# Gated linear recurrence and an ELU layer on one core: running products of decays with one score product per chunk, in place of a tree over queries and keys

## The chip, the cores and the metric

The kernel runs on one core of a Trainium2 chip. The metric is the device time in microseconds (us), as a median of runs; lower is better. Engines: PE is TensorE's matmul, PEld its weight load, DVE is VectorE, ACT is ScalarE, POOL is GpSimd, SP is SyncE, which issues the transfers.

## The reference

Four batches, eight heads, 768 tokens, a head of 48. A complex state per head decays by a complex factor at each token and takes up an outer product; the query reads its real part. The 3072 results of 384 then pass through a layer with an ELU and 2048 hidden columns. Inputs are float32, but the two weights come as float64, which the kernel turns into float32 itself.

```python
mag = np.sqrt(a_re * a_re + a_im * a_im)
scale = np.minimum(mag, 0.999) / (mag + 1e-06)
a_re_n, a_im_n = (a_re * scale, a_im * scale)
# ... cut: states start at zero
for t in range(S):
    ar, ai = (a_re_n[:, :, t, :, None], a_im_n[:, :, t, :, None])
    new_re = ar * S_re - ai * S_im
    new_im = ar * S_im + ai * S_re
    kv = np.einsum('bhd,bhe->bhde', k[:, :, t], v[:, :, t])
    S_re, S_im = (new_re + kv, new_im)
    y[:, :, t] = np.einsum('bhd,bhde->bhe', q[:, :, t], S_re)
# ... cut: x is y with heads side by side
h = x @ w_in
g = np.where(h > 0.0, h, alpha * (np.exp(np.minimum(h, 0.0)) - 1.0))
return (g @ w_out).astype(np.float32)
```

## The kernel before

Twelve groups of 256 tokens, two chunks of 128 each. Inside a chunk, a query at t and a key at s meet in exactly one block of 2, 4, .. 128 tokens that has s in its left half and t in its right half. At each of seven levels the kernel makes scores for those pairs, then widens queries (on DVE) and keys (on POOL) by the decays of the neighbouring block. Nothing is divided, so any decay is right.

```python
def product(eng, x, y_re, y_im, to_re, to_im, sign, shape, tag, seen=lambda t: t):
    # ... cut: buffers t1 and t2, signs
    eng.tensor_tensor(out=t1, in0=x, in1=y_re, op=ALU.mult)
    eng.tensor_tensor(out=t2, in0=x, in1=y_im, op=ALU.mult)
    eng.tensor_tensor(out=to_re, in0=seen(t1[:, 0]), in1=seen(t2[:, 1]), op=minus)
    eng.tensor_tensor(out=to_im, in0=seen(t1[:, 1]), in1=seen(t2[:, 0]), op=plus)

def widen(x, h):
    # ... cut: views of the chunk by blocks of h tokens
    product(nc.vector, qv, tot(0, 0), tot(1, 0), qv[:, 0], qv[:, 1], 1, shape, "pq")
    # ... cut: a new buffer for keys
    product(
        nc.gpsimd, old[:, :, 0], tot(0, 1), tot(1, 1), to[:, 0, 0], to[:, 1, 0], -1,
        shape, "pk", seen,
    )
    for i in range(2):
        nc.scalar.copy(out=to[:, i, 1], in_=seen(old[:, i, 1]))
    x["K"] = new

# ... cut: the order of a group; `behind` holds the ELU layer of the group before it
        for l, h in enumerate(LEVELS):
            for x in xs:
                scores(x, h)
                widen(x, h)
                if l % 2 or h == LEVELS[-1]:
                    values(x, l // 2)
            for w in weights[:4]:
                load_weights(*w)
            # ... cut
            if behind:
                behind.pop(0)()
```

## Time and profile before

| | before |
|---|---|
| time, median of the first 3 runs | 1701.91 us (1699.12 to 1703.77) |
| granted PE clock of the profiled run, mean | 0.819 |
| time per group of 256 tokens | 132 us, or 0.515 us a token |
| matmul records on PE | 10464 |
| table loads on ACT | 21 |

The page cuts the span into 40 equal slices, each digit being tenths of a slice in which the engine was busy. These are three engines' lines of the page of the kernel before:

```profile
PE   3522368948848847866876874894893893894989
...
DVE  7897888788788777867868868858858858858831
...
POOL 6574464665465464544654654645545645635610
```

A PE that alternates between 9 and 3 or 4 is one that stops once in every group. DVE is mostly at 7 or 8 and POOL at 4 to 6.

### The profile page before, as it was taken

To read this page: it belongs to the slowest core of one execution; us is meant where nothing else is said; L and a number is where in the kernel's file an instruction comes from. 1 tells how busy PE (TensorE), PEld (TensorE's weight loads), DVE (VectorE), ACT (ScalarE), POOL (GpSimd) and SP (SyncE) were. 2 spreads that over 40 slices of the span, in tenths; PEclk is the share of its full clock that TensorE was granted. 3 is DMA by queue.
4 is the path that set the end of the run, shared out by engine and by line. 5 is a ranking of instruction groups with operands and counts; after the bars stand their busy time and mean duration, and the time that the engine had idled before them with its cause. 6 is when DMAs were issued, how large, how long until landed. Compare 5 with 4: busy or idle time off the path is not lost.

```text
span 1704.6 us, 26958 instructions
## 1 busy us (share of the span) xinstructions
PE 1193.1 (70%) x10464; PEld 922.5 (54%) x10464; DVE 1289.6 (76%) x1860; ACT 439.2 (26%) x865; POOL 893.2 (52%) x835
## 2 busy tenths in 40 slices
PE   3522368948848847866876874894893893894989
PEld 2521355637637636655654653663662763773766
DVE  7897888788788777867868868858858858858831
ACT  2010043124124123122322331331421521311313
POOL 6574464665465464544654654645545645635610
PEclk8555679778978978987996996996895996996999
DMA  5413330030031040022022013013012012010000
GB/s 108 107 54 108 116 60 11 18 72 17 18 67 26 18 76 16 15 59 37 12 51 49 12 47 51 8 38 65 8 38 54 20 34 45 13 33 23 2 19 10
DMA packets 156895, 69.67 MB, mean 41 GB/s; under 512 B 134496, under 2 KB 142432, under 8 KB 156768
## 3 DMA queue, kind: packets, MB, share of 16 engines
q1 hardware_dynamic: 156768, 67.94, 17.8%
q8 instruction: 84, 1.38, 0.4%
q14 instruction: 43, 0.35, 0.1%
HBM read 36.44 MB, written 4.72 MB: 24 GB/s over the span
## 4 chain that ended last, share of the span: by engine, by line
PE 45%; DVE 44%; issue 4%; POOL 3%; ACT 2%; DMA 1%; SPq 1%; POOLq 0%; DVEq 0%
PE bank L414 15%; PE a L277 11%; DVE pq L248 8%; DVE pq L247 8%; PE bank L397 8%; PE y L304 6%; DVE T L250 4%; DVE T L251 4%; DVE Q L251 3%; DVE Q L250 3%; DVE r L192 3%; DVE a_sb L288 2%; DVE g L406 2%; POOL wp L172 2%; DVE Q L224 2%
## 5 line engine op out<-in xcount | busy, mean ns | idle before, releaser
L277 PE MATMUL a<-Q,K 48*64 48x128 f32 (+1 forms) x4992 | 350.6, 291 | 334.7 <-DVE Q L250 291.3
L277 PEld LDWEIGHTS a<-Q,K 48*64 48x64 f32 x4992 | 307.1, 149 | 387.5 <-issue 275.9
L250 POOL TENSOR_TENSOR K<-pk,pk 128x256 f32<-128x256 f32 x168 | 145.0, 863 | 408.0 <-PE a L277 400.4
L397 PE MATMUL bank<-x,w_in 128*128 128x256 f32 x1152 | 305.3, 421 | 13.2 <-ACT er L404 8.9
L332 ACT COPY K<-K 128x256 f32<-128x256 f32 x336 | 137.5, 445 | 566.6 <-PE a L277 492.1
L397 PEld LDWEIGHTS bank<-x,w_in 128*128 128x128 f32 x1152 | 232.9, 209 | 66.1 <-issue 22.8
L414 PE MATMUL bank<-w_out,g 128*128 128x384 f32 x768 | 267.0, 501 | 0.1
L247 POOL TENSOR_TENSOR pk<-K,T 128x512 f32<-128x512 f32 x168 | 208.6, 1242 | 67.8 <-DVE T L250 50.4
L248 POOL TENSOR_TENSOR pk<-K,T 128x512 f32<-128x512 f32 x168 | 231.0, 1375 | 0.0
L250 DVE TENSOR_TENSOR Q<-pq,pq 128x256 f32<-128x256 f32 x168 | 109.5, 652 | 131.7 <-PE a L277 126.0
L414 PEld LDWEIGHTS bank<-w_out,g 128*128 128x128 f32 x768 | 143.7, 193 | 98.9 <-issue 11.2
L304 PE MATMUL y<-a_sb,vl 128*64 128x128 f32 (+1 forms) x1344 | 119.5, 316 | 98.3 <-DVE a_sb L288 98.3
L248 DVE TENSOR_TENSOR pq<-Q,T 128x512 f32<-128x512 f32 x168 | 174.7, 1040 | 0.0
L247 DVE TENSOR_TENSOR pq<-Q,T 128x512 f32<-128x512 f32 x168 | 166.6, 992 | 3.9
L304 PEld LDWEIGHTS y<-a_sb,vl 128*64 128x64 f32 (+1 forms) x1344 | 94.3, 163 | 134.3 <-DVE a_sb L288 115.5
L406 DVE SCALAR_TENSOR_TENSOR g<-ee,er 128x512 f32<-128x512 f32 x96 | 85.5, 893 | 89.8 <-ACT ee L405 89.8
L251 POOL TENSOR_TENSOR K<-pk,pk 128x256 f32<-128x256 f32 x168 | 149.0, 887 | 0.0
L251 DVE TENSOR_TENSOR Q<-pq,pq 128x256 f32<-128x256 f32 x168 | 131.8, 785 | 0.0
L288 DVE TENSOR_TENSOR a_sb<-a,masks 128x1024 f32<-128x1024 f32 x72 | 87.4, 1214 | 55.7 <-PE a L277 55.7
L403 ACT ACTIVATE ee<-bank 128x512 f32<-128x512 f32 x96 | 57.1, 595 | 234.0 <-PE bank L397 179.6
L247 DVE TENSOR_TENSOR pq<-T 128x512 f32<-128x512 f32 (+6 forms) x168 | 100.5, 598 | 17.5 <-ACT T L219 12.4
L248 DVE TENSOR_TENSOR pq<-T 128x512 f32<-128x512 f32 (+6 forms) x168 | 97.3, 579 | 0.0
(68 smaller groups left out, 1261.2 us busy)
## 6 DMA issues: line engine op xcount, KB each, us to landing
w<-in_moe_w_in_dram SPq DMA_DIRECT2D x12, 512.0 KB
vl<-vn SPq DMA_DIRECT2D x48, 128.0 KB
vl<-vn SPq DMA_DIRECT2D x96, 64.0 KB
vl<-vn SPq DMA_DIRECT2D x192, 32.0 KB
w<-in_moe_w_out_dram SPq DMA_DIRECT2D x16, 384.0 KB
ar<-in_a_re_dram SPq DMA_DIRECT2D x24, 192.0 KB
ai<-in_a_im_dram SPq DMA_DIRECT2D x24, 192.0 KB
kn<-in_k_dram SPq DMA_DIRECT2D x24, 192.0 KB
```

The source lines that it names most:

```text
L247: eng.tensor_tensor(out=t1, in0=x, in1=y_re, op=ALU.mult)
L248: eng.tensor_tensor(out=t2, in0=x, in1=y_im, op=ALU.mult)
L250: eng.tensor_tensor(out=to_re, in0=seen(t1[:, 0]), in1=seen(t2[:, 1]), op=minus)
L251: eng.tensor_tensor(out=to_im, in0=seen(t1[:, 1]), in1=seen(t2[:, 0]), op=plus)
L277: nc.tensor.matmul(x["a"][ts(row, HP), z, ts(p, n)], lhsT=x["K"][rows, i, ts(p, C // 2)], rhs=x["Q"][rows, i, ds((p + 1) * C - n, n)], sta ...
L288: nc.vector.tensor_tensor(out=a, in0=x["a"].rearrange("p j (x t) -> p j x t", t=C), in1=masks[:, n].unsqueeze(1).unsqueeze(1).to_broadcast ...
L304: nc.tensor.matmul(to, **got, start=False, stop=False, skip_group_check=True)
L332: nc.scalar.copy(out=to[:, i, 1], in_=seen(old[:, i, 1]))
L397: nc.tensor.matmul(t[:, e], lhsT=w_in[:, i, ts(f0 + f + e, C)], rhs=x[:, i], start=(i == 0), stop=(i == NI - 1),)
L403: nc.scalar.activation(out=e, in_=t, func=AF.Relu, scale=-1.0)
L406: nc.vector.scalar_tensor_tensor(out=g[:, f : f + 2], in0=e, scalar=-1.0, in1=r, op0=ALU.add, op1=ALU.add)
L414: nc.tensor.matmul(t, lhsT=gs[f // FB][:, f % FB, ts(c, C)], rhs=w_out[:, f], start=(f == 0), stop=(f == NF - 1),)
```

## The change

The intent is to replace the tree by running products. Within a group of now 384 tokens the kernel computes P, the product of all decays up to each token (divided by powers of 0.905, the middle of the expected range, so that it stays near 1). The decay between s and t is P at t over P at s. Queries are multiplied by P, keys divided by it, and one ordinary 96 by 96 score product per head and chunk replaces seven levels. Three neighbouring tokens lie on one partition: P is first multiplied within the triples, then over 128 triples by a doubling scheme in transposed form (`across`), then turned back (`back`).

Division is only safe while P stays in range. The kernel therefore looks at the squared size of P at every eighth triple, keeps the smallest and the largest, and after the loop a branch runs a plain token-by-token version if either left its bounds. Other parts of the change: all products move to DVE, POOL keeps one addition per weight tile and some small fills, and 1/|a| is made by Ln and Exp instead of Sqrt and a reciprocal.

```diff
-C = 128  # tokens of a chunk, the length over which decays are multiplied out
-LEVELS = [1, 2, 4, 8, 16, 32, 64]
+J = 3
+NB = 128
+GT = J * NB
+CB = 32
+C = J * CB
+BASE = 0.905
 # ... cut: normalising, of a third of a group (j)
-        nc.scalar.activation(out=m, in_=m, func=AF.Sqrt)
-        nc.vector.reciprocal(out=r, in_=r)
+                nc.scalar.activation(out=y, in_=s, func=AF.Ln)
+                nc.scalar.activation(out=y, in_=y, func=AF.Exp, scale=-0.5)
+                nc.scalar.activation(out=t, in_=y, func=AF.Square)
+                nc.scalar.activation(out=s, in_=y, func=AF.Ln, scale=2.0 / CAP * EPS, bias=1.0)
+                nc.scalar.activation(out=s, in_=s, func=AF.Exp, scale=-1.0)
 # ... cut: running products over 128 triples, four DVE instructions per level and block
-    def widen(x, h):
+            def across(levels):
+                Z = x["Z"]
+                for h in levels:
+                    o = Z[:, :, :, 1:].rearrange("p i m (n s b) -> p i m n s b", s=2, b=h)
+                    for m in range(NI):
+                        product(r, tot, r, shape, "u")
+            def back():
+                nc.vector.tensor_tensor(out=low, in0=low, in1=s[:, 0], op=ALU.min)
+                nc.vector.tensor_tensor(out=high, in0=high, in1=s[:, 0], op=ALU.max)
+                X = nat["X"] = sb.tile(flat, FP32, tag="X", name="X")
+                for i in range(2):
+                    t = bank([NB, HD])
+                    for m in range(NI):
+                        nc.tensor.transpose(t[:, ts(m, 128)], Z[:, i, m, 0:NB], ident)
+                    nc.scalar.mul(out=X[:, i], in_=t, mul=place)
 # ... cut: queries_keys(j): queries times P, keys times conj(P) / |P|^2, both transposed
-    def scores(x, h):
+        def attend(x, c, state, y_sb, last):
+                    nc.tensor.matmul(
+                        sc[:, e], lhsT=K[:, h + e, ts(c, C)], rhs=Q[:, h + e, ts(c, C)],
+                        start=True, stop=True,
+                    )
 # ... cut: the order of a group; `behind` is the ELU layer of the group before,
 # `ahead` the preparation of the next one, in four chunks of which the last is `late`
+                late = c == NC - 1
+                for s in behind if late else behind[:5]:
+                    s()
+                behind = behind[5:]
+                for s in ahead if late else ahead[:3]:
+                    s()
+                ahead = ahead[3:]
 # ... cut: at the end
+    general(tc, cst, ident, w_in, w_out, low, high, q, k, v, a_re, a_im, out)
```

## The prediction

> **What bounds the kernel now.** I read the page's head first, for the load of each engine, then its chain, then groups kept apart by shape, and last stretches of the timeline.
>
> ```profile
> PE 1193.1 (70%) x10464; PEld 922.5 (54%) x10464; DVE 1289.6 (76%) x1860; ACT 439.2 (26%) x865; POOL 893.2 (52%) x835
> ...
> PEclk8555679778978978987996996996895996996999
> ...
> PE 45%; DVE 44%; issue 4%; POOL 3%; ACT 2%; DMA 1%; SPq 1%; POOLq 0%; DVEq 0%
> ```
>
> No engine is full. The chain that ends last is half TensorE (PE) and half VectorE (DVE): they hand work to each other level by level, and PE's granted clock drops while it waits. The groups by shape:
>
> ```profile
> L277 PE MATMUL a<-Q,K 48*64 48x128 f32 x4224 | 319.6, 302 | 334.7 <-DVE Q L250 291.3 <-DVE Q L224 28.0 <-DVE Q L251 14.8
> L248 DVE TENSOR_TENSOR pq<-Q,T 128x512 f32<-128x512 f32 x168 | 174.7, 1040 | 0.0
> L248 POOL TENSOR_TENSOR pk<-K,T 128x512 f32<-128x512 f32 x168 | 231.0, 1375 | 0.0
> ```
>
> The third number after the bar is idle time ahead of the group and who ended it: PE idles 335 us ahead of the tree's scores, 291 of it for DVE's query products. Why those are slow shows in three timeline rows of DVE:
>
> ```profile
> 43.65 0.69 DVE L247 TENSOR_TENSOR pq<-T 128x512 f32<-128x512 f32 x1
> 384.00 0.15 DVE L251 TENSOR_TENSOR T<-pq,pq 128x4 f32<-128x4 f32 x1
> 399.25 1.75 DVE L248 TENSOR_TENSOR pq<-Q,T 128x512 f32<-128x512 f32 x1
> ```
>
> The same 512 elements take 0.69 us while GpSimd (POOL) is idle and 1.75 us while it works on keys. The two clean rows give a law: 0.15 us + 1.04 ns per element (384: 0.55 us, as the state row of the last group has). The period of the loop is in the chain in order of time; the rows are three groups of 256 tokens apart:
>
> ```profile
> 479.06 1.93 PE y L343 x32
> ...
> 874.82 1.93 PE y L343 x32
> ...
> 1270.84 1.93 PE y L343 x32
> ```
>
> That is 396 us for three, 132 us a group, 0.515 us a token.
>
> **What the Trainium skill says.** (1) "SBUF — State Buffer": the port pair that DVE and GpSimd share is an exclusive lock, and a DVE instruction with two SBUF inputs contends with a GpSimd one that reads SBUF. The trace agrees (0.69 against 1.75 us). (2) "ScalarE: Activation LUTs", What ACT_TABLE_LOAD costs: about 1283 ns, plus a drain of 1380 ns. The trace has 21 loads of 1283 ns, but the next activation starts at once, so I count 1.28 us. (3) The same page, Table sets: one set holds Exp and Ln. The changed build's instruction listing nevertheless has a load between almost every Ln and Exp. (4) "TensorE: Matmul & The Clock Gate", Part 1: idling halves the PE clock. The trace agrees: 16 value matmuls take 1.09 us warm and 1.95 us after an idle time of 4.7 us.
>
> **The change, part by part.** Counts are from the listing of the two builds' instructions. A float32 matmul appears in the trace as two records.
>
> *Removed.* All 24 trees: 4992 score records (64 take 3.69 us warm, so 288 us of PE), 1536 value records, DVE's query products and POOL's key products (168 x 4 each), 336 key copies on ACT, 12 reciprocals of 4.94 us, and 528 small transfers that sort values. POOL keeps only 34 additions in the weight conversion, about 45 us instead of 893. So from the first group on, DVE has the lock to itself.
>
> *PE after.* The two MLP products stream the same columns: 768 + 768 records of 384 columns, 32 of them in 10.52 us, so 0.329 us each, 253 + 253 us. Attention: 512 score records of 96x96, 448 state updates, 512 values, 448 state reads. From the warm paces of similar shapes (0.036 to 0.064 us where halves of the array alternate; I take 0.1 us where the whole array is used) this is 51 + 40 + 26 + 22 us. 480 transposes at 0.136 us (8 in 1.09) are 65 us. Sum 710 us warm, 89 us in each of eight groups of 384 tokens.
>
> *DVE after,* by the law: 40 complex products of 768 (3.0 us each) 120; 168 products of 128 along the chunk totals (1.0 us) 168; normalising 24 x 3.15 = 76; the rest of queries and keys 24 x 4.1 = 98; masks, states and elu, 220 of 384 elements, 121; weights 34 conversions 88; rest 8. Sum 679 us instead of 1290: 74 us a group, and the weights once.
>
> *ACT after.* Activations by the rows of before (768: 0.84, 512: 0.585, 384: 0.48 us) 349 us; table loads: 137 outside the token-by-token path, x 1.28 = 176 us. Sum 525, 66 us a group; up from 439.
>
> *Stages.* The listing fixes each engine's order, so I walk it.
> - Prologue, nothing beside it: loads 5; normalising, bound by ACT with its loads, 25; products within triples 6; transposes 2; 21 chained products 20; back 2; queries and keys 26. About 86 us.
> - First group: DVE carries its 63 us and some 25 weight conversions of 2.7 us: 130 us.
> - A middle group has three phases. Attention with normalising: ACT has some 37 us (nine to ten loads, 12 of the MLP's tiles), 38 with handoffs. Chained products: DVE 24 us, PE 29 with 15 projection matmuls. Then the listing puts 16 projection matmuls (10.5 us) between the fifth and the sixth transpose of the running products, so DVE waits about 11; queries and keys follow, 10.5 us for the first chain and 7 for each further one, 26. Sum 104 us, 0.27 us a token instead of 0.515.
> - Six such: 624. Last group without preparation, PE bound: 85. Last MLP alone: 32 + 32 + 5 = 69. Range check and branch at the end: 5; with these data the token-by-token path must not be taken: the reference draws a_re from 0.85 to 0.95 and a_im with spread 0.1, so log |a| spreads by about 0.033 a token around log 0.905, over 768 tokens by 0.033 x 27.7 = 0.9, and the check's bounds lie at 8.3.
>
> 86 + 130 + 624 + 85 + 69 + 5 = 999 us. Handoffs not walked and cold clock come on top; before, the busiest engine's load was 76% of the span, and 710 of 999 would be 71%. I add 5%: **1050 us**.
>
> **The rivals.**
> (a) *ACT's table loads become the bound.* For: 137 loads instead of 21, inside the serial chain of normalising (four per step) and ahead of the MLP's Exp, which frees PE's banks. Against: ACT's 66 us a group is less than PE's 89. If half of the 17 loads of a group stop everything beyond what I counted, six groups lose 6 x 8.5 x 1.28 = 65 us: 1115.
> (b) *PE stays warm and overlap is better.* For: the MLP's matmuls fill every phase and the loop would approach PE's 89 us: 999 - 6 x 15 = 910. Against: the fixed order with the projection ahead of the last transpose.
> (c) *The weights bind the start.* 12.6 MB of double words at the 108 GB/s of the page's first slices are 117 us, which is hidden under 86 + 130 us, if slots come free in time: nine slots, freed by DVE. If not, 30 to 60 us more.
> (d) *The fallback runs.* It has 768 serial steps: the time would be many times longer. I give it 1%.
>
> **Range and chances.** (a) and (c) together reach 1180, (b) most of the way 950: 8 in 10 between 950 and 1180. Faster by over 2% needs below 1668 us, far outside all but (d): faster 0.97, same 0.01, slower 0.02.
>
> **What would show it.** In the changed profile: POOL under 60 us and no 512-element DVE product above 0.7 us (lock); DVE busy 640 to 720, PE 750 to 950 (its busy time counts latency and cold clock), ACT 500 to 550 with 137 loads of 1283 ns; a period near 104 us between the same instruction of neighbouring groups; a DVE wait of about 11 us ahead of the first query product in each group, ended by ACT's copy of the running products; PE idle and cold in the first 200 us. It is wrong if the period is nearer 90 (b) or 120 (a), if the first group passes 270 us (c), or if DVE's short strided products cost more than the law says.

## The result, and the profile after

The changed kernel is correct and takes **1070.65 us** (median of four runs, 1064.39 to 1073.67) where the kernel before, over four runs, takes 1702.84 us (1699.12 to 1706.22). The ratio is 0.628, with a 95% interval of 0.626 to 0.630. Ratios here and below are the mean time of one kernel's runs over that of the other's from the same rounds, so not quite the ratio of the medians quoted.

The page of the kernel after, in the same parts as before: load, slices with the granted clock, and the chain by engine.

```profile
PE 790.0 (74%) x3938; PEld 508.9 (48%) x3938; DVE 603.4 (57%) x1568; ACT 534.2 (50%) x813; POOL 46.6 (4%) x78
...
PE   0037303246899689978897789878987799899998
...
DVE  2887858875483648555746575636754684421120
ACT  8162160049721975189418952696249723631330
POOL 0003303310000000000000000000000000000000
PEclk9997555668799869988899899988998999899999
...
PE 40%; ACT 22%; issue 17%; DVE 15%; POOL 3%; DMA 2%; SPq 0%; POOLq 0%; ACTq 0%; DVEq 0%
```

PE's records fell from 10464 to 3938, DVE's time halved, and POOL is silent after a quarter of the span. PE is mostly idle over the first fifth, and its clock falls to 5 there; from there on it is busy but not full. (The low clock of that start decides nothing: in the control p0, below, the first group shows a clock of 0.92 instead of 0.63 and takes 171.6 us instead of 169.5.) What is new is ACT: it was 2% of the chain that ended last and is now 22%. Its line now climbs to 7, 8 or 9 once in each group and falls back to 1 or 2 in between.

The groups by shape show that what remains of DVE's products runs at the undisturbed pace, and where ACT's time goes:

```profile
L425 DVE SCALAR_TENSOR_TENSOR g<-e,h 128x384 f32<-128x384 f32 x128 | 70.3, 550 | 148.4 <-ACT e L424 148.2
...
L168 DVE TENSOR_TENSOR u<-Z 128x128 f32<-128x128 f32 x168 | 48.7, 290 | 6.5 <-ACT Z L243 2.1
L295 ACT COPY K<-bank 96x512 f32<-96x512 f32 x48 | 38.1, 855 | 8.8 <-PE bank L292 8.7
...
L322 ACT ACT_TABLE_LOAD x24 | 30.8, 1283 | 0.4
L211 ACT ACT_TABLE_LOAD x23 | 29.5, 1283 | 14.5 <-DVE s L208 14.1
...
L169 DVE TENSOR_TENSOR t<-P,X 128x768 f32<-128x768 f32 x24 | 22.8, 952 | 61.2 <-ACT X L285 61.2
```

Products of 768 elements take 0.95 us and those of 128 take 0.29 us, both within 0.01 us of 0.15 us + 1.04 ns per element. Two of the eight lines that carry table loads are shown; all eight hold 137 loads, 176 us. The last line shows a DVE wait of 61.2 us, to which the timeline of one group belongs:

```profile
659.84 0.71 PE L284 MATMUL bank<-ident,Z 128*128 128x128 f32 x5
...
660.42 0.59 ACT L285 ACTIVATE X<-bank,place 128x384 f32<-128x384 f32 x1
...
660.57 10.59 PE L432 MATMUL o<-w_out,g 128*128 128x384 f32 x32
...
671.00 0.27 PE L284 MATMUL bank<-ident,Z 128*128 128x128 f32 x1
...
671.57 0.59 ACT L285 ACTIVATE X<-bank,place 128x384 f32<-128x384 f32 x1
...
672.19 0.96 DVE L169 TENSOR_TENSOR t<-P,X 128x768 f32<-128x768 f32 x1 [10.20 <-ACT X L285]
```

PE makes five of six transposes of P, then 32 projection records, then the sixth transpose. ACT's second copy of P and DVE's second product wait for it 10.2 us, six times in the program.

ACT in the busy part of the same group, by its own timeline:

```profile
713.15 1.28 ACT L211 ACT_TABLE_LOAD   x1
714.45 0.52 ACT L211 ACTIVATE y<-s 128x384 f32<-128x384 f32 x1
714.99 1.28 ACT L212 ACT_TABLE_LOAD   x1
716.28 0.52 ACT L212 ACTIVATE y<-y 128x384 f32<-128x384 f32 x1
716.84 0.52 ACT L213 ACTIVATE t<-y 128x384 f32<-128x384 f32 x1
```

Line 211 is Ln and line 212 Exp. Each has its own load, and an activation of 0.52 us costs 1.8 us with it. From 689 to 731 us ACT is busy for 40.6 of 42 us, and 14 loads, 18 us, lie in that stretch.

For the stages I marked each group by the instruction that squares P for the range check, once per group, and asked for busy times between marks. The columns are: from and to, length, busy time (and instructions) of each engine, granted clock, share of the transfers' engines, GB/s. For the kernel after, the rows are the prologue, the first group, a middle group, and the rest after the last mark:

```profile
0.00:57.30 57.30, 3.02 (x11) 1.94 (x11) 33.10 (x112) 24.80 (x31) 0.60 (x12) 1.00 0.48 127
57.30:226.80 169.50, 54.13 (x314) 42.14 (x315) 133.37 (x360) 51.16 (x71) 43.22 (x38) 0.63 0.30 82
656.00:767.60 111.60, 97.47 (x495) 61.66 (x494) 65.33 (x167) 67.39 (x102) 0.58 (x6) 0.91 0.21 49
877.80:1067.00 189.20, 177.38 (x757) 106.92 (x755) 44.29 (x81) 61.77 (x108) 0.00 (x0) 0.98 0.07 21
```

A middle group takes 111 us (two of them, from 656.00 to 877.83 us, take 221.8), 0.29 us a token. PE is busy for 97.5 of 111.6 us with a clock of 0.91, so it is close to the bound, but no engine is full. Two reasons are in view, the order of the sixth transpose and the table loads; the experiments separate them.

### The profile page after: what moved, and what is told of

Its sections match the earlier page's. It is cut to its first block, busy times and chain, and to the rows that moved or that the text cites. A ratio compares the mean times of both kernels' runs of the same rounds, so it can differ in the third digit from the quotient of the medians.

```text
span 1067.0 us, 11388 instructions
## 1 busy us (share of the span) xinstructions
PE 790.0 (74%) x3938; PEld 508.9 (48%) x3938; DVE 603.4 (57%) x1568; ACT 534.2 (50%) x813; POOL 46.6 (4%) x78
## 3 DMA queue, kind: packets, MB, share of 16 engines
q1 hardware_dynamic: 109360, 55.17, 20.5%
## 4 chain that ended last, share of the span: by engine, by line
PE 40%; ACT 22%; issue 17%; DVE 15%; POOL 3%; DMA 2%; SPq 0%; POOLq 0%; ACTq 0%; DVEq 0%
PE h L416 17%; PE o L432 13%; POOL wp L156 3%; PE sc L356 3%; PE bank L368 2%; PE y L375 2%; ACT L217 2%; ACT L212 2%; ACT L323 2%; ACT K L295 2%; ACT L211 1%; ACT L322 1%; DVE wp L153 1%; PE y L382 1%; DVE wf L146 1%
## 5 line engine op out<-in xcount | busy, mean ns | idle before, releaser
L416 PE MATMUL h<-x,w_in 128*128 128x384 f32 x768 | 310.1, 546 | 44.8 <-DVE g L425 39.5
L432 PE MATMUL o<-w_out,g 128*128 128x384 f32 x768 | 257.5, 492 | 1.3 <-ACT o L437 1.1
L416 PEld LDWEIGHTS h<-x,w_in 128*128 128x128 f32 x768 | 148.0, 209 | 151.2 <-DVE g L425 64.4
L432 PEld LDWEIGHTS o<-w_out,g 128*128 128x128 f32 x768 | 145.7, 191 | 106.4 <-ACT o L437 7.7
L425 DVE SCALAR_TENSOR_TENSOR g<-e,h 128x384 f32<-128x384 f32 x128 | 70.3, 550 | 148.4 <-ACT e L424 148.2
L423 ACT ACTIVATE e<-h 128x384 f32<-128x384 f32 x128 | 62.1, 486 | 135.7 <-PE h L416 89.1
L356 PEld LDWEIGHTS sc<-Q,K 96*96 96x96 f32 x512 | 59.0, 192 | 20.0 <-ACT K L295 8.7
L424 ACT ACTIVATE e<-e 128x384 f32<-128x384 f32 x128 | 66.8, 521 | 3.2
L356 PE MATMUL sc<-Q,K 96*96 96x96 f32 x512 | 61.8, 279 | 6.6 <-ACT K L295 6.5
L169 DVE TENSOR_TENSOR t<-P,X 128x768 f32<-128x768 f32 x24 | 22.8, 952 | 61.2 <-ACT X L285 61.2
L168 DVE TENSOR_TENSOR u<-Z 128x128 f32<-128x128 f32 (+1 forms) x172 | 49.3, 287 | 6.5 <-ACT Z L243 2.1
L169 DVE TENSOR_TENSOR u<-Z 128x128 f32<-128x128 f32 (+1 forms) x172 | 48.3, 281 | 0.0
```

The lines of the kernel that those rows point to most:

```text
L168: nc.vector.tensor_tensor(out=t1, in0=x, in1=y[0], op=ALU.mult)
L169: nc.vector.tensor_tensor(out=t2, in0=x, in1=y[1], op=ALU.mult)
L356: nc.tensor.matmul(sc[:, e], lhsT=K[:, h + e, ts(c, C)], rhs=Q[:, h + e, ts(c, C)], start=True, stop=True,)
L416: nc.tensor.matmul(t, lhsT=w_in[:, i, ts(f, 128)], rhs=x[:, i], start=(i == 0), stop=(i == NI - 1),)
L423: nc.scalar.activation(out=e, in_=t, func=AF.Relu, scale=-1.0)
L424: nc.scalar.activation(out=e, in_=e, func=AF.Exp, scale=-1.0)
```

## The experiments

All were timed in three rounds beside the kernel before. All of them are correct except b1 and b2.

| run | what | median us | ratio to before |
|---|---|---|---|
| after | the change | 1070.65 | 0.628 |
| b1_keys_still | before, keys not widened | 1419.06 | 0.833 |
| b2_both_still | before, keys and queries not widened | 1213.06 | 0.712 |
| p0_small7 | after, one small buffer fewer (control) | 1071.46 | 0.629 |
| p1_pool_busy | p0 + useless products on POOL | 1252.88 | 0.735 |
| p2_pool_busy_free | p1, small fills moved off POOL | 1212.30 | 0.712 |
| e1_one_set | after + one table set chosen at the start | 905.51 | 0.531 |
| e2_back_first | after, `back` ahead of the projection | 1035.06 | 0.608 |
| e2b_prep_first | after, all preparation ahead of it | 1021.14 | 0.600 |
| e4_no_check | after, without range check and branch | 1070.04 | 0.628 |
| e5_set_prep | e1 + e2b | 886.46 | 0.520 |
| e6_set_prep_dve | e5, weights' addition on DVE | 877.73 | 0.515 |
| e7_weights_spread | e6, four weight tiles a chunk, not seven | 882.65 | 0.518 |

### Where the gain came from: the tree taken apart

b1 removes the keys' part of `widen` from the kernel before, so the levels below use keys that are not widened. It gives wrong results (relative error 1.74) on the same shapes.

```diff
-        product(
-            nc.gpsimd, old[:, :, 0], tot(0, 1), tot(1, 1), to[:, 0, 0], to[:, 1, 0], -1,
-            shape, "pk", seen,
-        )
-        for i in range(2):
-            nc.scalar.copy(out=to[:, i, 1], in_=seen(old[:, i, 1]))
-        x["K"] = new
```

> The kernel before with its keys left unwidened (wrong result on purpose): GpSimd's 672 key products and ACT's 336 copies go, TensorE and VectorE keep every instruction. Theory (a good part of the 632 us came from the shared port: VectorE's two-input operations wait for GpSimd): mean of the 512-element query product falls from about 1.02 to 0.70 us, VectorE busy from 1290 to 950 to 1050 us, time from 1703 to 1350 to 1500 us. Rival (the level-by-level handoff between TensorE and VectorE sets the pace, whatever GpSimd does): 1600 us or more.

Measured: 1419.06 us (1413.13 to 1421.24). Of the groups by shape, the tree's scores, ahead of which PE idled for 334.7 us before, and the query product, which took 1.04 us on average before:

```profile
L277 PE MATMUL a<-Q,K 48*64 48x128 f32 x4224 | 300.2, 290 | 180.1 <-DVE Q L250 161.8 <-DVE Q L224 11.5 <-DVE Q L251 6.1
...
L248 DVE TENSOR_TENSOR pq<-Q,T 128x512 f32<-128x512 f32 x168 | 118.2, 703 | 0.0
```

With POOL not multiplying keys, the same instruction takes 0.70 us, near the 0.69 us that the timeline before showed while POOL was idle. DVE's busy time falls from 1289.6 to 916.0 us although b1 has as many DVE instructions (1860); 950 to 1050 had been expected. About half of PE's wait for queries is left (180.1 us). The 284 us are an upper bound for this contention, since b1 also takes POOL's own chain and 336 copies away from ACT.

b2 takes the query product out as well (relative error 5.01).

```diff
-        qv = x["Q"].rearrange("p a (n s i) -> p a n s i", s=2, i=h)[:, :, :, 1]
-        product(nc.vector, qv, tot(0, 0), tot(1, 0), qv[:, 0], qv[:, 1], 1, shape, "pq")
```

> As b1, with the queries left unwidened too (wrong result on purpose): VectorE's 672 query products go as well; TensorE keeps all its 10464 records. Theory: TensorE's own warm pace, about 1060 us, becomes the bound: 1120 to 1250 us, so what remains down to 1070 us is TensorE work that the change removed. Rival (masks, totals, start and MLP handoffs bound the rest): 1300 us or more.

Measured: 1213.06 us (1208.87 to 1215.54). The head of its page:

```profile
PE 1065.7 (88%) x10464; PEld 846.9 (70%) x10464; DVE 581.1 (48%) x1188; ACT 308.6 (25%) x531; POOL 168.2 (14%) x163
```

Now PE alone holds the time: from 600 to 1000 us it was busy for 384.5 of 400 us at a clock of 1.00. PE was busy for 1065.7 us in all, so even a tree whose widening cost nothing and which never let PE wait would take about as long as the changed kernel does (an estimate from that busy time). The changed kernel, with 6526 records fewer, needs PE for 790.0 us. Read in this order, the gain is 284 us for the keys, 206 us for the queries (1419 to 1213) and 142 us for the rest (1213 to 1070.65), PE work above all; another order could share it out differently. The last step is a net one: b2 also still has the masks, the reciprocals and the small transfers that the change drops, and the changed kernel has new costs of its own. None of these was timed alone.

### Is an undisturbed DVE part of the gain in the new kernel?

If so, giving POOL useless work should take time back. The buffer for it needed space, so p0 is the control that frees it.

```diff
-SMALL, GB = 8, 9
+SMALL, GB = 7, 9
```

> Control for p1: the changed kernel with one buffer fewer (7 instead of 8) of the small tiles, which makes room for p1's output tile; the TensorE order is identical. Expected by all: within 1.5% of 1070 us.

Measured: 1071.46 us (1071.21 to 1072.17); the control costs nothing. p1 adds 16 products of 384 columns per chunk from the second group on, 448 in all, whose result nobody reads.

```diff
+                if n:
+                    for f in range(NF):
+                        nc.gpsimd.tensor_tensor(out=idle, in0=w_out[:, f], in1=w_out[:, 0], op=ALU.mult)
```

> p0 with 448 useless two-input GpSimd products of 384 elements beside the groups after the first, on no other engine's path (TensorE order identical). Theory (VectorE free of the lock is part of the gain): flat 768-element products rise from 0.95 us to 1.3 us or more, VectorE busy from 603 by 100 to 250 us, time by 60 to 180 us. Rival (VectorE idles 43% of the span, so slower operations are absorbed): VectorE busy rises but the time stays within 2% of p0.

Measured: 1252.88 us (1249.18 to 1254.90), 181 us over the control, 1 us more than the 60 to 180 us expected. It is not a clean answer: POOL also fills small paddings of real tiles, and these fills now queue behind the useless products; the timeline shows one PE wait of 52.10 us for such a fill. p2 moves the fills to DVE.

```diff
-            nc.gpsimd.memset(t[:, HD:], 0.0)
+            nc.vector.memset(t[:, HD:], 0.0)
-                    nc.gpsimd.memset(Z[:, 0, :, 0:1], 1.0)
-                    nc.gpsimd.memset(Z[:, 1, :, 0:1], 0.0)
+                    nc.vector.memset(Z[:, 0, :, 0:1], 1.0)
+                    nc.vector.memset(Z[:, 1, :, 0:1], 0.0)
```

> As p1, but the small fills that stood in GpSimd's queue behind the useless products (padding of values, first decay of a sequence) are done by VectorE, since p1 showed one wait of 52 us of TensorE for such a fill. TensorE order the same but for 68 of 2302 places. Theory (lock): p1 without that wait, 1190 to 1215 us, the periods of the groups with a busy GpSimd again 36 to 42 us longer than the changed kernel's. Rival (p1's loss was mostly its queue): below 1110 us.

Measured: 1212.30 us (1211.41 to 1213.95), 141 us over the control. Its groups by shape, to be held against those of the kernel after:

```profile
L168 DVE TENSOR_TENSOR u<-Z 128x128 f32<-128x128 f32 x168 | 89.4, 532 | 6.4 <-ACT Z L243 2.4
...
L425 DVE SCALAR_TENSOR_TENSOR g<-e,h 128x384 f32<-128x384 f32 x128 | 69.9, 547 | 111.1 <-ACT e L424 110.8
...
L168 DVE TENSOR_TENSOR t<-P,X 128x768 f32<-128x768 f32 x24 | 32.1, 1339 | 9.8 <-ACT X L285 9.8
```

The products with both inputs in SBUF slow from 0.29 to 0.53 us and from 0.95 to 1.34 us. The second of each pair of short products, which follows the first at once, stays at 0.30 us. The trace, read instruction by instruction, shows why: of the first products, 70 start while a POOL product runs, and take 0.88 us on average; those that start while none runs take 0.28 to 0.29 us on average. Of the second products, 64 start just before the next POOL product does, and take 0.28 us. Whichever starts first is not delayed. The ELU's operation `g`, which has one input in PSUM, is as fast as ever (0.55 us). That agrees with what the Trainium skill's page "SBUF — State Buffer" (section "Who interferes with whom") says of the ports that both engines share (a DVE operation with two SBUF inputs contends with a GpSimd one that reads SBUF), and it excludes a general slowing of DVE. The marks agree: the four groups from the second to the fifth take 137.0, 147.6, 149.2 and 128.8 us, together 562.5 against 429.3 in p0 (40, 34, 41 and 19 us longer, where 36 to 42 had been expected of each), and once POOL's queue is empty the period is 109 to 110 us again. So an undisturbed DVE is part of the gain in the new kernel too. How much it is worth depends on POOL's load: the useless products keep POOL busy for 528 us, the kernel before kept it busy for 893 us.

### What holds the changed kernel: table loads

Theory: the 137 table loads lie in the serial chains of ACT, DVE and PE. Rival: ACT has slack (534 of 1067 us), and the order ahead of the sixth transpose holds the loop. e1 adds one line at the start, which loads the set that has both Ln and Exp.

```diff
+    nc.scalar.preload_act_table_set("natural_log_exp_and_others")
     w_in = cst.tile([128, NI, DF], FP32, name="w_in")
```

> The changed kernel with one line added: the activation table set that serves both Ln and Exp is loaded once at the start; the TensorE order of the build is identical (2302 of 2302 instructions), the 137 loads become 1. Theory (the loads sit in the chain that sets a group's period): the loads fall from 136 to 0 in the groups, 14 of a group's 17 lie in a 42 us stretch in which ACT never idles, 4 in the serial query-key chain; the period falls from 110.8 us by 14 to 18 us to 93 to 97 us, the prologue by about 20 us (16 loads x 1.28), the whole to 945 to 975 us. Rival (ACT's 66 us a group is beside TensorE's 90, so the loads are hidden; only the prologue gains): 1045 to 1055 us.

Measured: **905.51 us** (902.83 to 905.68), correct. The gain, 165 us, is larger than expected (945 to 975 us). In the two traces, PE's order of instructions is the same; apart from the loads, ACT's differs in 13 of 678 places and DVE's in 21 of 1570. One load is left, and the stages become:

```profile
0.00:43.90 43.90, 3.05 (x11) 1.98 (x12) 32.87 (x112) 11.87 (x21) 0.60 (x12) 1.00 0.63 166
43.90:198.60 154.70, 55.94 (x314) 43.64 (x315) 133.35 (x360) 30.33 (x55) 43.09 (x38) 0.58 0.32 90
541.40:631.90 90.50, 88.48 (x495) 56.93 (x494) 64.92 (x167) 43.40 (x85) 0.58 (x6) 1.00 0.25 60
722.20:903.30 181.10, 174.72 (x757) 105.00 (x755) 44.12 (x81) 53.59 (x102) 0.00 (x0) 1.00 0.07 21
```

A middle group loses 17 loads (ACT goes from 102 instructions to 85) and 20.5 us (the last two periods are 110.9 and 90.4 us on average): 1.2 us for each load of 1.283 us, although ACT's busy time was only half of the span. That the loads hold the period is shown; that nearly every one of them stood on the path is not. PE needs less time for the same matmuls: it was busy for 97.5 of 111.6 us at clock 0.91 and is now for 88.5 of 90.5 us at clock 1.00 (97.5 x 0.91 is 88.7). So in that group some 9 of the 21 us gained come with PE's clock, which stays up once PE no longer waits, and 12 are the waits themselves. PE is now full. The timeline of ACT in e1 shows the same Ln, Exp and Square back to back, without a load.

```profile
586.41 0.52 ACT L212 ACTIVATE y<-s 128x384 f32<-128x384 f32 x1
586.96 0.52 ACT L213 ACTIVATE y<-y 128x384 f32<-128x384 f32 x1
587.52 0.52 ACT L214 ACTIVATE t<-y 128x384 f32<-128x384 f32 x1
```

(Its line numbers are one higher.) Loads also delay the ELU, whose Exp frees PE's banks: PE's wait ahead of the first MLP product for DVE's `g` falls from 39.5 to 5.4 us.

### What holds the changed kernel: the order ahead of the sixth transpose

e2 puts `back` ahead of the projection in the last chunk of a group. e2b puts all the preparation there.

```diff
                 late = c == NC - 1
+                if late and ahead:
+                    ahead.pop(0)()
                 for s in behind if late else behind[:5]:
```

> The changed kernel with only the emission order changed: the transposes of the running products are emitted ahead of the previous group's projection, so they are not held behind 16 projection matmuls. Theory (the 10.2 us that DVE waits for the second half of X, once a group, is on the path, and TensorE has slack for the projections elsewhere): the period falls by 6 to 10 us, the whole to 1000 to 1030 us. Rival (the projections are only moved and ACT's loads still fill the next stage, so the wait reappears elsewhere): within 1% of 1070 us.

Measured: 1035.06 us (1032.61 to 1041.50), just outside the range expected. The waits for P (61.2 and 23.0 us before the two products) are gone, and 36 of about 84 us are gained. Part of the rest comes back as PE's wait for ACT's copy of `o`, ahead of the projection (L432): 35.4 us in e2, 1.1 us in the changed kernel. That ACT's table loads are what delays this copy is likely, but no run shows it.

```diff
                 late = c == NC - 1
+                if late:
+                    for s in ahead:
+                        s()
+                    ahead = []
                 for s in behind if late else behind[:5]:
```

> As e2_back_first, but all of the next group's queries and keys are emitted ahead of the projection, so the projections become filler between them. Theory: as e2_back_first or some 5 us a group better, since TensorE idles about 11 us a group in that stage: 970 to 1020 us. Rival: the projections then delay the next attention chunk instead: 1050 to 1090 us.

Measured: 1021.14 us (1020.39 to 1027.23), again just outside the range. The groups by shape of e2b, the line that had 61.2 us of wait:

```profile
L169 DVE TENSOR_TENSOR t<-P,X 128x768 f32<-128x768 f32 x24 | 22.8, 952 | 0.0
```

The order is real, and worth 50 us while the loads stay. e5 has both changes, e1 and e2b.

> e1 and e2b together. If the two waits are in series in a group, the gains add: period about 85 to 92 us, near TensorE's own 89 us of work, whole 890 to 930 us. If they are alternatives (either shadows the other), it is no better than the better of the two by more than 1%.

Measured: **886.46 us** (886.11 to 887.04), better than expected. The gains do not add: 165 and 50 us alone, 184 together. After the loads are gone, the order is worth 19 us only (905.51 to 886.46), because PE has little idle time left to win (2 of 90.5 us in a middle group of e1); in e1 the DVE wait of 10.2 us is still there in six groups, 61.2 us in all, and costs no more than these 19. So the result lies between the two readings that the expectation allowed, waits in series and waits in each other's shadow. In e5 the middle group takes 87 to 88.5 us, of which PE is busy for all but half a microsecond:

```profile
528.30:615.40 87.10, 86.69 (x494) 56.43 (x494) 65.58 (x168) 45.02 (x85) 0.58 (x6) 1.00 0.26 62
```

### The range check

```diff
-    general(tc, cst, ident, w_in, w_out, low, high, q, k, v, a_re, a_im, out)
```

> The changed kernel without the range check's last step and without the token-by-token path (the running bounds are still kept). Theory: the branch costs what stands behind the last output transfer, 0 to 5 us: 1065 to 1071 us. Rival (the larger program or the load of the flag costs more than the 5 us of the prediction): 1055 us or less.

Measured: 1070.04 us (1068.84 to 1071.27), against 1070.65 us for the whole change. No cost is seen; the spread of the runs is larger than the difference. In the trace of the changed kernel the last output copy starts at 1062.74 us and the check's matmul at 1063.27 us, beside the last transfer. The build without the branch also shows that nothing of the slow path runs with these data, and the result is correct.

### The first group

The first group between its marks takes 169.5 us in the changed kernel, with a DVE that is busy for 133 us. One step of each weight tile is an addition on POOL between two DVE steps. e6 is e5 with that addition on DVE.

```diff
-            nc.gpsimd.tensor_tensor(out=p, in0=p, in1=f, op=ALU.add)
+            nc.vector.tensor_tensor(out=p, in0=p, in1=f, op=ALU.add)
```

> e5 with the addition in the weight conversion on VectorE in place of GpSimd (34 x 0.55 us more on VectorE, no lock and no handoff). Theory: the start of e5 (first 198 us) is VectorE with waits for GpSimd's 1.25 us additions; it gets 5 to 20 us shorter: 866 to 881 us. Rival (VectorE is full there, the added work cancels it): 884 to 892 us.

Measured: **877.73 us** (876.95 to 878.07), ratio 0.515: this is the fastest version, ahead of the kernel before and of the change. The second mark moves from 198.53 us in e5 to 187.26 us. 34 additions more on DVE cost less than the handover to POOL and back.

e7 spreads the weights: four tiles per chunk instead of seven, in the hope that the first group is bound by them and later groups have room.

```diff
-                for w in weights[:7]:
+                for w in weights[:4]:
                     load_weights(*w)
-                weights = weights[7:]
+                weights = weights[4:]
```

> e6 with four instead of seven weight tiles converted per chunk, so that nine of them move from the first group into the second, where VectorE has room. Theory (the first group is bound by VectorE): another 10 to 24 us: 845 to 870 us. Rival (the slots that hold double words are then taken by the MLP's tiles, so the conversions wait and TensorE with them): the same as e6 or slower.

Measured: 882.65 us (880.49 to 884.11), slower by 5 us. The hoped-for range was missed. The theory held for the first group: DVE is busy for 114.7 of its 117.8 us, and the second mark comes 25 us earlier (161.98 us). But the second group then takes 102.8 us where it took 76.5 us (187.26 to 263.74), and all of it is given back. DVE, which now converts there, is busy for 88.6 us of it instead of 65.4; which wait ends last there was not looked up.

## Why the prediction was right, and where it was not

The time is 2% above the prediction and well inside its range. Its mechanism held: the lock, PE's load and the wait at the sixth transpose. That the number is so close is in part luck, since the 5% (50 us) on top of 999 us had no named cause, and what it covered were two misses of 39.5 and 27.0 us. Its sum can be laid beside the marks, if the prologue's last parts (back 2, queries and keys 26) are counted after the mark, as in the trace:

| stretch | predicted us | measured us |
|---|---|---|
| start to first mark | 86 - 28 = 58 | 57.3 |
| first group | 28 + 130 - 28 = 130 | 169.5 |
| six middle groups | 624 | 651.0 |
| rest (28 of the last preparation, 85, 69, 5) | 187 | 189.2 |
| sum | 999 | 1067.0 |

- **The lock: right.** POOL's busy time was predicted under 60 us and is 46.6. No group of products of two SBUF inputs is over 5% slower than the law (there are none of 512 elements left, for which it named 0.7 us). One of its rows was misread: POOL was not at the keys beside DVE's 1.75 us at 399.25 us, but at the product for the diagonal (`vd`, line 230 of the kernel before). The row ahead of it, 1.53 us at 397.79 us, did run beside a key product, so the reading stands. p2 shows that the law breaks when POOL is kept busy, and what that costs (141 us).
- **PE: right.** 750 to 950 us predicted, 790.0 measured. The 89 us a group worked out from warm durations is the floor that e1 and e5 reach (90.4 us in the last two groups, 88.0 us in the last three). One term is off: 448 state updates at 0.1 us are 45 us, not 40.
- **DVE: too large.** 679 us predicted, 603.4 measured, below the 640 to 720 that it named. Each shape took the time that the law gives it: its groups by shape add up to 688 us. What the sum missed is that instructions in a row overlap a little, so that the engine is busy for less than the sum. In the timeline, a product at 673.19 us is given 0.56 us, but the next starts 0.47 us later. With 1568 instructions, 76 us are 0.05 us each.
- **ACT: right in total, by two errors that cancel.** 525 us predicted, 534.2 measured. Its groups by shape add up to 556 us, and overlap in a row takes 22 us off again. The 96 copies of 96 by 512 were sized at 0.585 us and took 0.85 us, 26 us more. They scatter into every third token; whether that is the cause was not tested.
- **The wait at the sixth transpose: right.** About 11 us predicted, 10.20 us measured, in six groups. But its gain does not add to that of the loads, as e5 shows.
- **The first group: the step that failed most.** "DVE carries its 63 us and some 25 weight conversions of 2.7 us: 130 us." DVE was indeed busy for 133.4 us, so its work was sized right. The step took DVE to be full, and it idled for 36 us. 15 of the 39 us missing go with the table loads (169.5 to 154.7 in e1) and 11 with the handover of the weights' addition to POOL (154.6 in e5 to 143.4 in e6). In e6 DVE is busy for 138.7 of 143.4 us, so there the step holds: the remaining 13 us are 9 us more DVE work than 130, the additions moved to it included, and 5 us of idle DVE. The rival that weights bind the start was half right: no DVE wait in that group ends with a transfer, but the conversion is a chain through two engines.
- **Middle groups: 108.5 us on average instead of 104.** The first of the six takes 97.2 us, the other five 110.8, which is nearer to 104 than to the 120 at which the prediction called itself wrong. The mis-sized term is most likely the stretch that ACT bounds: the walk gave it some 37 us with nine to ten loads; in the trace, the stretch in which ACT is full has 14 loads in 42 us (it also holds the end of the queries and keys). Taking all 17 loads of a group away gained 20.5 us (e1). The rival that ACT's loads bind was thus true in kind; the size it was given (65 us on top) was too large, because most of the loads were counted in the walk already. The other rival, a loop near PE's 89 us (910 us), is what e1 makes of the kernel (905.51 us).
- **The fallback: right.** It did not run. The check was put at 5 us, and e4 shows no cost.

## What to carry to other kernels

Read an engine's place in the serial chain before its share of the span: ACT was half idle, yet taking 136 of its 137 table loads away (176 us) gained 165 us, a part of it by PE's clock. When two waits are found in one loop, try them together as well as alone, since the second is worth only what the next full engine leaves (50 us alone, 19 us after the first). And before optimising a tree's handoffs, take the work that is handed over out, wrong results and all, and see what the engine that remains takes (1213 us here): this tells whether to mend the algorithm or to replace it.

## What the Trainium skill lacked or had wrong

- **"ScalarE: Activation LUTs", section "Table sets: the hidden batching unit".** It says that Ln followed by Exp is one table load, as one set has both. In the build of the changed kernel it is a load for nearly every switch, 137 in all, since nothing told the build to use that set. Choosing the set once at the start left one load and took 165 us off (1070.65 to 905.51). The page's rules say to use that set where both are needed, but not what makes a build use it.
- **The same page, section "What ACT_TABLE_LOAD costs".** It adds a drain of about 1380 ns to the load of about 1283 ns. The load is 1283 ns in every trace here, but the drain is not seen: a load starts at 714.99 us, the next activation at 716.28 us, and each load removed from a middle group gave 1.2 us.
- **"SBUF — State Buffer", section "Who interferes with whom".** The page says which pairs of operations exclude each other and that the later one blocks fully; for two streams side by side it gives only two ratios, 6.8 and 1.5, without the shapes. Here, beside GpSimd products of 1.18 us in a row, one product of 384 on VectorE took up to 1.34 us instead of 0.55 us (line 214 of p2, at 445.56 us), and the averages went from 0.95 to 1.34 us (768 elements) and from 0.29 to 0.53 us (the first of two products of 128), while the second of the two, which mostly started ahead of the next GpSimd product, stayed at 0.30 us. That an operation with an input in PSUM is spared (0.55 us in both) agrees with the page.
- **"TensorE: Matmul & The Clock Gate".** I found no pace for float32 matmuls there ("FP8 and Floating Point Precision", section "TensorE Precision Notes", says that a true float32 product takes four passes, and a footnote of "Perfetto Trace Analysis", section "Engine Utilization", halves the array's output rate for FP32_LOW_HIGH; neither gives a matmul's time). The runs show two records for each; warm, with 384 columns, a record takes 0.33 us (32 in 10.59 us).
- **No page that I found** gives a figure for a ScalarE copy out of PSUM whose destination is scattered: 0.855 us for 96 by 512 elements into every third token, against 0.585 us in the kernel before for 128 by 512 elements into a dense tile.
